# One layer half of the first group spread behind the second group's attention, in a fused gated-attention and layer kernel

## The chip, the cores and the metric

The kernel runs on one core of a Trainium2 chip. A core has a matrix engine (TensorE, PE in the profile; its weight loads are listed apart as PEld), a vector engine (VectorE, DVE), an engine for functions of one argument (ScalarE, ACT), GpSimd (POOL) and a queue engine (SyncE, SP) that here only issues DMAs. Each engine works through its own queue in order, and engines wait for one another through semaphores. The metric is the device time of one execution in microseconds; less is better.

## The reference

Two parts follow one another. The first is a recurrence over 768 steps for each of 4 x 8 heads of width 48: a complex state with a per-channel decay, written by k and v and read by q. The second is a layer over the 3072 rows that come out of it.

```python
mag = np.sqrt(a_re * a_re + a_im * a_im)
scale = np.minimum(mag, 0.999) / (mag + 1e-06)
a_re_n, a_im_n = (a_re * scale, a_im * scale)
for t in range(S):
    new_re = ar * S_re - ai * S_im
    new_im = ar * S_im + ai * S_re
    S_re, S_im = (new_re + np.einsum('bhd,bhe->bhde', k[:, :, t], v[:, :, t]), new_im)
    y[:, :, t] = np.einsum('bhd,bhde->bhe', q[:, :, t], S_re)
# x: y as 3072 rows of 384
h = x @ w_in            # 384 x 2048
g = h * np.cos(h)
out = g @ w_out         # 2048 x 384
```

All arrays are float32 but for the two weight matrices, which come as float64.

## The kernel before

**Tiles and groups.** The recurrence is computed in chunks of 128 steps. Two chunks make a group, and there are 12 groups, numbered from 0 (so that group 0 is the first). In a group, logarithms of the decays are summed along the chunk by a matmul with a triangular matrix, and their exponentials scale q and k. Angles are summed in the same way and give sines and cosines. Then a chunk is an ordinary masked attention (`f_scores`, `f_out`, L931 and L943) and a carried state (`f_state`, L984).

**The steps of a group, by their names in the code.**

- `log_steps` (L731): 3 logarithms and 3 exponentials on ScalarE, and sums and products on VectorE. It writes the tiles `lg`, `tan`, `mag` and `rs`.
- `p_powers` (L790): the matmuls `lgs` and two exponentials for each chunk; `p_even` and `p_apply` (L802, L830): five VectorE products, and a small DMA pair through `row`.
- `g_angle` (L836): an arctangent; `g_carry` (L844): only from group 2 on, the carry of the angle and its split into two halves.
- `g_phase` (L855): the matmuls `phs`, a cast on ScalarE and a subtraction on VectorE for each chunk. In groups 0 and 1 the second chunk's matmuls read the first chunk's finished phase.
- `g_trig` and `g_stack` (L869, L882): two sines, and four products that give `ks` and `qs`.
- Group 1 turns `ks` and `qs` by TensorE transposes (`f_turn`, L914, tiles `tp`). From group 2 on VectorE transposes them (`f_transpose`, L894), and a DMA through DRAM (`moved`) brings them to `kT` and `qT`.
- `f_xt` (L1003) brings the attention's output `yT` through DRAM into `xT`, the layer's input.

**The layer.** Its first half, `mm1(g, jp)`, is eight tiles of 128 x 512 a group (`hp`, 12 matmul records each). ScalarE takes a sine with a quarter turn (`gate`) and a square whose sum is kept as a check (`junk`), and VectorE multiplies: `gate` = hp cos(hp). The second half, `mm2`, multiplies the gates by `w_out` into `op`. Groups 0 and 1 do it plainly, 16 matmuls (32 records) for each of two chunks; `second(g, i)` (L1198) cuts them into four quarters. Later groups use seven products of sums in place of eight.

**The weights.** Each matrix is brought in eight parts (`into` for `w_in`, `back` for `w_out`) by DMAs that POOL issues, and turned from float64 to float32 by `as_floats` (L621): one ScalarE and three VectorE instructions a part. Four staging buffers `raw` take turns in the pool `stage`, which is closed (`room.close()`) once all parts are there. A quarter of `second` needs two parts of `w_out`.

**Buffers.** PSUM has eight banks: five in turn under the tag `a` (scores, sums, transposes), two under `m` and one under `acc` (layer). Each third `hp` tile of a group goes to `acc`. There are eight `gate` buffers.

**What sets the order.** All matmuls are chained in the order in which the code calls them, and so are ScalarE's functions that need a table (`special`, L704, which also places the table loads), the squares of the logs, and POOL's DMAs. The other instructions of VectorE and ScalarE and the DMAs on SP are placed by a planner when the program is built: among those that are ready by its own costs, the one that the code calls first. `weave` (L1140) orders the calls: each list of steps gets a stretch of 0 to 1, its steps are spread evenly over it, and all are called by position. The start (to about 45 us) is written out by hand; then come two `weave` calls for groups 0 and 1, the closing of `stage`, one more `weave`, and a loop over the other groups.

Of the kernel before, what the change touches and what calls it, by code (L numbers as in the profile page):

```python
# [11 lines left out]
F32 = mybir.dt.float32  # L12
# [475 lines left out]
def fast_path(ctx, tc, q, k, v, a_re, a_im, moe_w_in, moe_w_out, out, least, odd, wide):  # L488
# [8 lines left out]
    DM, DF = moe_w_in.shape  # L497
    C = 128
    NCH = S // C
    G = 2  # L500
# [7 lines left out]
    NJ = DF // C  # L508
# [7 lines left out]
    msb = ctx.enter_context(tc.tile_pool(name="msb", bufs=2))  # L516
# [3 lines left out]
    stage = {"pool": room.enter_context(tc.tile_pool(name="stage", bufs=1)), "bufs": 4}  # L520
    pa = ctx.enter_context(tc.tile_pool(name="pa", bufs=5, space=PSUM))
    pm = ctx.enter_context(tc.tile_pool(name="pm", bufs=3, space=PSUM))
# [20 lines left out]
    X = [dict() for _ in range(NG)]  # L543
    Y = [dict() for _ in range(N)]

    PEG, PER = 2, 1

    def load(g, names, i=None, put=nc.sync.dma_start):  # L550
        for name in names:
            ap = {"re": a_re, "im": a_im, "q": q, "k": k, "v": v}[name]
            if name not in X[g]:
                X[g][name] = ld.tile([C, G, H, D], F32, tag=name, name=name,
                                     bufs=2 if name == "v" else 1)
            b, c = divmod(g * G + (i or 0), NCH)
            one, n = i or 0, G if i is None else 1
            steps = ap[b].rearrange("h (c p) d -> p c h d", p=C)[:, ds(c, n)]
            tile_ = X[g][name][:, ds(one, n)]
            parts = [(0, C, 0)]  # L560
            if name in ("re", "im") and g >= PEG:

                parts = [(0, C - 16, 1), (C - 16, C - 1, 1)]
                put(out=tile_[C - 1:C], in_=steps[0:1])
            for i_ in range(n):
                for lo, hi, by in parts:
                    put(out=tile_[lo:hi, i_], in_=steps[lo + by:hi + by, i_])

    idle = stage["pool"].tile([C, 512], F32, name="idle")
    nc.vector.memset(idle, 1.0)  # L570
    for names in ("re", "im"), ("k", "q"), "v":
        for i in range(G):
# [15 lines left out]
    RAW = stage["bufs"]  # L588
# [115 lines left out]
    def special(func, **kw):  # L704
        preload(tables[func])
        chain(nc.scalar.activation(func=func, **kw))  # L706
# [4 lines left out]
    def temp(tag, bufs=1):  # L711
        return gt.tile([C, G * DM], F32, tag=tag, name=tag, bufs=bufs)
# [5 lines left out]
    def cut(t, i, n):  # L718
        return (flat(t) if len(t.shape) == 4 else t)[:, ds(i * DM, n * DM)]
# [70 lines left out]
    def p_powers(g, i):  # L790

        x = X[g]
        if i == 0:
            x["P"], x["Q"] = x["lg"], temp("Q")
            x["row"] = rows_d.tile([G * DM], F32, tag="row", name="row")
            x["end"] = ft.tile([D2, G * H], F32, tag="end", name="end")
        ps = pa.tile([C, DM], F32, tag="a", name="lgs")
        summed_up(ps, g, i, "lg", sums[0])
        special(out=cut(x["P"], i, 1), in_=ps, func=AF.Exp)
        special(out=cut(x["Q"], i, 1), in_=ps, func=AF.Exp, scale=-1.0)  # L800
# [35 lines left out]
    def g_angle(g, i, n):  # L836

        at = cut(X[g]["tan"], i, n)
        special(out=at, in_=at, func=AF.Arctan)
# [172 lines left out]
            out=xt.rearrange("p c g t -> p c (g t)"),  # L1012
            in_=moved.rearrange("p s d t -> (p s d) t").rearrange("(c r) t -> r c t", r=C))

    def mm1(g, jp):
        x = X[g]
        third = len(x.setdefault("gate", {})) % 3 == 2
        ps = pm.tile([C, 2, G * C], F32, tag="acc" if third else "m", name="hp",
                     bufs=1 if third else 2)
        for ji in range(2):  # L1020
            for dc in range(ND):
                matmul(ps[:, ji], lhsT=w_in[:, jp, dc, ts(ji, C)],
                       rhs=x["xT"][:, dc].rearrange("p g t -> p (g t)"),
                       start=(dc == 0), stop=(dc == ND - 1))
        gate = msb.tile([C, 2, G * C], F32, tag="gate", name="gate", bufs=8)
        junk = msb.tile([C, 2, G * C], BF16, tag="junk", name="junk", bufs=1)
        special(out=gate, in_=ps, func=AF.Sin, scale=1.0 / in_scale, bias=half_pi_b)
        scalar.activation(out=junk, in_=ps, func=AF.Square, scale=1.0 / in_scale,
                          accum_out=wide[:, ds(g * (NJ // 2) + jp, 1)])
        gated = vector.tensor_tensor(out=gate, in0=ps, in1=gate, op=ALU.mult)  # L1030
        x.setdefault("gated", gated)
        x["gate"][jp] = gate

    def mm2(g, i, j0, nj):
        if j0 == 0:
            Y[g * G + i]["op"] = pm.tile([C, DM], F32, tag="acc" if i == 0 else "m", name="op",
                                         bufs=1 if i == 0 else 2)
        ps = Y[g * G + i]["op"]
        for j in range(j0, j0 + nj):
            matmul(ps, lhsT=X[g]["gate"][j // 2][:, j % 2, ts(i, C)], rhs=w_out[:, j],  # L1040
                   start=(j == 0), stop=(j == NJ - 1))
        if j0 + nj == NJ:
            ot = msb.tile([C, DM], F32, tag="ot", name="ot")
            scalar.mul(out=ot, in_=ps, mul=1.0 / (in_scale * out_scale))
            nc.sync.dma_start(out=out[ts(g * G + i, C), :], in_=ot)
# [1 line left out]

    PLAIN, HJ, E2 = 2, NJ // 2, DM // 2  # L1050
    b11, b12, b21, b22 = (w_out[:, ds(r * HJ, HJ), ds(c * E2, E2)]
                          for r in range(2) for c in range(2))
    right = {"a11": b11, "a12": b21, "s3": b12, "s4": b22}
# [86 lines left out]
    def weave(*parts):  # L1140

        items = []
        for p, (part, lo, hi) in enumerate(parts):
            part = list(part)
            items += [(lo + (hi - lo) * (i + 0.5) / len(part), p, t)
                      for i, t in enumerate(part)]
        for _, _, t in sorted(items, key=lambda x: x[:2]):
            t()
# [4 lines left out]
    def keys(g):  # L1153

        if not 0 <= g < NG:
            return
        for i, n in spans(g):
            yield lambda i=i, n=n: g_trig(g, i, n)
            yield lambda i=i, n=n: (g_stack(g, i, n), p_end(g, i, n))
            for name in "kT", "qT":  # L1160
                if g >= PEG:
                    yield lambda i=i, n=n, name=name: f_transpose(g, i, n, name)

    def turned(g, i, name):
        return [lambda hh=hh: f_turn(g, i, name, hh) for hh in range(2)]

    def prods(g):
        if not 0 <= g < NG:
            return
        for i in range(G):  # L1170
            yield lambda i=i: p_powers(g, i)
        yield lambda: g_angle(g, 0, G)
        yield lambda: g_carry(g)
        yield lambda: (p_even(g, 0, G), p_apply(g, 0, G))

    def logs(g):
        yield from each(g_log, g)
        if 0 <= g and g + 1 < NG:
            yield lambda: load(g + 1, ("re", "im"))

    def phases(g):
        return [lambda i=i: g_phase(g, i) for i in range(G)] if 0 <= g < NG else []

    def chunks(g):
        for n in range(g * G, g * G + G):
            for hh in range(2):
                yield lambda n=n, hh=hh: f_scores(n, hh)
            yield lambda n=n: f_state(n)
            yield lambda n=n: f_out(n)
        yield lambda: f_xt(g)  # L1190
        if g + 2 < NG:
            yield lambda: load(g + 2, ("k", "q", "v"))

    def first(g):
        order = range(NJ // 2) if g < PLAIN else (0, 4, 1, 5, 2, 6, 3, 7)
        return [lambda jp=jp: mm1(g, jp) for jp in order]

    def second(g, i):  # L1198
        return [lambda j0=j0: mm2(g, i, j0, 4) for j0 in range(0, NJ, 4)] if g < PLAIN else []

    def convert(parts):
        return [lambda dst=dst, src=src: weight(dst, src)() for dst, src in parts]
# [12 lines left out]
    into, back = weight_parts()  # L1215
# [35 lines left out]
    for t in (turned(0, 0, "kT") + turned(0, 0, "qT") + early[:1]  # L1251
# [6 lines left out]
              + [lambda: next(one, None), lambda: next(two, None),  # L1258
                             lambda: load(2, ("v",))]):
        t()  # L1260
    weave((logs(1), 0.0, 0.1), (convert(into[RAW:]), 0.0, 0.5),
          (first(0), 0.2, 1.0), (prods(1), 0.55, 0.58), ([lambda: load(2, ("k", "q"))], 0.58, 0.6),
          (phases(1), 0.7, 0.8), (keys(1), 0.8, 0.9), (convert(back[:4]), 0.5, 1.0))
    over = [t for i in range(G) for name in ("kT", "qT") for t in turned(1, i, name)]
    weave((convert(back[4:]), 0.0, 0.3), (second(0, 0), 0.0, 0.65), (over, 0.2, 0.6),
          (logs(2), 0.3, 0.31), (chunks(1), 0.7, 1.0), (prods(2), 0.85, 0.87))
    room.close()
    stage.update(pool=ctx.enter_context(tc.tile_pool(name="late", bufs=1)), bufs=1)
    weave((second(0, 1), 0.0, 0.35), (phases(2), 0.2, 0.3), (keys(2), 0.3, 0.45),
          (first(1), 0.4, 1.0))  # L1270
    for n in range(2, NG):
        weave((mixes(n - 1, 2, 4), 0.0, 0.12), (logs(n + 1), 0.0, 0.02), (chunks(n), 0.0, 0.36),
              (second(n - 1, 0), 0.0, 0.38), (products(n - 1, 0, 3), 0.0, 0.36),
# [82 lines left out]
```

## Time and profile before

| what | us |
|---|---|
| median of three runs (lowest, highest) | 675.45 (675.18, 677.47) |
| the profiled execution | 674.87 |
| its span, first to last instruction | 673.0 |
| TensorE busy | 649.9 (97%) |
| VectorE busy | 490.5 (73%) |
| ScalarE busy | 396.5 (59%) |
| 26 table loads on ScalarE, 1283 ns each | 33.4 |

The profile is of one execution. Busy time is what an engine spends in its instructions; it overlaps between engines. In a line of instructions, `out<-in` are the program's tile names, followed by shapes and the count; in brackets stands the idle time of the engine just before, and the instruction that ended it. Most instructions carry the line of a helper that issues them (L686 for matmuls, L675 for VectorE and ScalarE, L706 for `special`), so the tile names tell them apart. One matmul in the code is two records in the trace (a transpose is one). The length of an instruction overlaps with the start of the next one on its engine, so that a row of equal ones is counted by its pitch.

### The profile page before, as it was taken

To read this page: it belongs to the slowest core of one execution; us is meant where nothing else is said; L and a number is where in the kernel's file an instruction comes from. 1 tells how busy PE (TensorE), PEld (TensorE's weight loads), DVE (VectorE), ACT (ScalarE), POOL (GpSimd) and SP (SyncE) were. 2 spreads that over 40 slices of the span, in tenths; PEclk is the share of its full clock that TensorE was granted. 3 is DMA by queue.
4 is the path that set the end of the run, shared out by engine and by line. 5 is a ranking of instruction groups with operands and counts; after the bars stand their busy time and mean duration, and the time that the engine had idled before them with its cause. 6 is when DMAs were issued, how large, how long until landed. Compare 5 with 4: busy or idle time off the path is not lost.

```text
span 673.0 us, 10725 instructions
## 1 busy us (share of the span) xinstructions
PE 649.9 (97%) x4055; PEld 579.6 (86%) x4055; DVE 490.5 (73%) x793; ACT 396.5 (59%) x730; POOL 27.8 (4%) x47
## 2 busy tenths in 40 slices
PE   7897899999999999999999999999999999999995
PEld 5685677886899889999899999999999999999895
DVE  4989987668867867877768778868778768862241
ACT  6779875483574575476477467467467467332330
POOL 2012000000000000000000000000000000000000
PEclk8989989999999999999999999999999999999998
DMA  9788725814824845955945864864864862363000
GB/s 252 162 244 234 188 67 116 215 41 87 220 58 92 214 119 122 230 119 118 234 119 118 216 136 117 214 138 116 218 141 116 215 140 87 115 143 105 24 6 24
DMA packets 232810, 94.90 MB, mean 141 GB/s; under 512 B 208798, under 2 KB 221217, under 8 KB 232748
## 3 DMA queue, kind: packets, MB, share of 16 engines
q1 hardware_dynamic: 226252, 68.62, 45.2%
q0 software_dynamic: 5632, 25.17, 11.4%
q8 instruction: 34, 0.56, 0.3%
q10 hardware_dynamic: 864, 0.33, 0.2%
q14 instruction: 28, 0.23, 0.1%
HBM read 69.28 MB, written 24.81 MB: 140 GB/s over the span
## 4 chain that ended last, share of the span: by engine, by line
PE 80%; ACT 6%; DVE 6%; DMA 6%; issue 2%; SPq 0%; ACTq 0%; DVEq 0%
PE hp L686 32%; PE op L686 17%; PE sum L686 14%; PE yp L686 6%; PE sc L686 5%; PE sp L686 3%; PE phs L686 2%; DMA re<-in_a_re_dram 1%; PE lgs L686 1%; ACT raw L675 1%; DMA qT<-moved 1%; DMA raw<-in_moe_w_in_dram 1%; DVE mag L675 1%; DMA raw<-in_moe_w_out_dram 1%; DVE tan L675 1%
## 5 line engine op out<-in xcount | busy, mean ns | idle before, releaser
L686 PE MATMUL hp<-xT,w_in 128*128 128x256 f32 x1152 | 253.1, 381 | 1.3 <-DVE gate L675 0.9
L686 PEld LDWEIGHTS hp<-xT,w_in 128*128 128x128 f32 x1152 | 219.9, 191 | 33.3 <-DVE gate L675 1.8
L706 ACT ACTIVATE gate<-hp,half_pi_b 128x512 f32<-128x512 f32 x96 | 65.9, 687 | 127.6 <-PE hp L686 127.6
L686 PE MATMUL op<-w_out,gate 128*128 128x192 f32 (+1 forms) x448 | 103.7, 377 | 3.1 <-DVE w_out L675 3.1
L675 DVE TENSOR_TENSOR gate<-hp,gate 128x512 f32<-128x512 f32 x96 | 65.7, 685 | 55.8 <-ACT junk L675 55.8
L686 PEld LDWEIGHTS op<-w_out,gate 128*128 128x128 f32 x448 | 75.9, 191 | 19.7 <-DVE w_out L675 4.1
L675 ACT ACTIVATE junk<-hp 128x512 bf16<-128x512 f32 x96 | 56.5, 589 | 0.0
L686 PE MATMUL sum<-t_s,s 128*128 128x192 f32 x320 | 55.4, 327 | 0.0
L686 PEld LDWEIGHTS sum<-t_s,s 128*128 128x128 f32 x320 | 52.5, 191 | 0.3 <-DVE ot L675 0.3
L675 DVE TENSOR_TENSOR atm<-sc,causal 128x512 f32<-128x512 f32 x48 | 32.8, 687 | 24.8 <-PE sc L686 24.8
L686 PE MATMUL sc<-qT,kT 96*128 96x128 f32 x384 | 49.3, 276 | 1.4 <-ACT qT L675 0.8
L686 PEld LDWEIGHTS sc<-qT,kT 96*128 96x128 f32 x384 | 47.8, 192 | 3.2 <-ACT qT L675 1.1
L675 ACT ACTIVATE ot<-sum 128x192 f32<-128x192 f32 x30 | 9.5, 319 | 49.8 <-PE sum L686 49.8
L702 ACT ACT_TABLE_LOAD x26 | 33.4, 1283 | 4.0 <-DMA ident<-ident_const 3.6
L675 DVE SCALAR_TENSOR_TENSOR ot<-op,ot 128x192 f32<-128x192 f32 x31 | 11.0, 355 | 32.5 <-ACT ot L675 23.9
L675 ACT CAST tan<-phs 128x384 int32<-128x384 f32 x24 | 11.5, 478 | 39.2 <-PE phs L686 39.2
L686 PE MATMUL yp<-atm,v 128*48 128x128 f32 x352 | 33.6, 277 | 0.0
L686 PEld LDWEIGHTS sp<-v,ks 128*96 128x96 f32 x320 | 29.7, 165 | 0.0
L686 PE MATMUL yp<-qT,state 96*48 96x128 f32 x304 | 29.7, 272 | 0.0
L686 PE MATMUL sp<-v,ks 128*96 128x48 f32 x320 | 29.6, 246 | 0.0
L686 PE MATMUL sum<-w_out,gate 128*128 128x192 f32 x160 | 29.6, 329 | 0.0
L686 PE MATMUL op<-t_a,gate 128*128 128x192 f32 x160 | 29.0, 333 | 0.0
(138 smaller groups left out, 997.2 us busy)
## 6 DMA issues: line engine op xcount, KB each, us to landing
moved<-tr SPq DMA_DIRECT2D x20, 768.0 KB
raw<-in_moe_w_in_dram POOLq DMA_DIRECT2D x16, 768.0 KB, 5.8
raw<-in_moe_w_out_dram POOLq DMA_DIRECT2D x16, 768.0 KB, 4.7
kT<-moved SPq DMA_DIRECT2D x40, 192.0 KB
qT<-moved SPq DMA_DIRECT2D x10, 768.0 KB
k<-in_k_dram SPq DMA_DIRECT2D x24, 192.0 KB
q<-in_q_dram SPq DMA_DIRECT2D x24, 192.0 KB
v<-in_v_dram SPq DMA_DIRECT2D x24, 192.0 KB
```

Source lines behind the costliest of these rows:

```text
L675: ins = getattr(self.engine, op)(**kw)
L686: chain(nc.tensor.matmul(out, **kw), "tensor")
L702: chain(nc.scalar.preload_act_table_set(table))
L706: chain(nc.scalar.activation(func=func, **kw))
```

## The change

Four edits, all in the order of the work for groups 0 and 1 (41 to 140 us of the kernel before):

- `mm1` is cut in two, `mm1_sums` (matmuls) and `mm1_gate` (ScalarE and VectorE). For group 0 four tiles' sums are called ahead, three of them before group 1's powers; gates follow after group 1's arctangent. Strings of letters say which PSUM bank each tile takes (`m`, `c` for `acc`, `a`).
- The powers of group 1 are called right behind its logs, and its two phases directly behind one another, behind two gates.
- The first four gates of group 0 have four buffers of their own in the pool `stage`, the first of them shared with the constant tile `idle` of the start. `op` of both chunks of group 0 takes the bank `acc`.
- Of `second(0, 0)` the first quarter is called between the transposes of group 1's two chunks, the second in the middle of group 1's attention, and the other two after it. Seven parts of `w_out` are converted along that attention, one before it. `second(0, 1)` comes between the halves of `first(1)`, and `stage` is closed after all of this.

```diff
-    PEG, PER = 2, 1
+    PEG, PER, PLAIN = 2, 1, 2
...
-    idle = stage["pool"].tile([C, 512], F32, name="idle")
+    idle = stage["pool"].tile([C, 2, G * C], F32, tag="first", name="idle", bufs=4)
+    idle = idle.rearrange("p a b -> p (a b)")
...
-    def mm1(g, jp):
-        x = X[g]
-        third = len(x.setdefault("gate", {})) % 3 == 2
-        ps = pm.tile([C, 2, G * C], F32, tag="acc" if third else "m", name="hp",
-                     bufs=1 if third else 2)
+    def mm1_sums(g, jp):
+        x = X[g]
+        x.setdefault("gate", {})
+        order = x.setdefault("order", [])
+        home = {0: "mmcamcmm", 1: "mmmmmmcm"}[g][jp] if g < PLAIN else "mmc"[len(order) % 3]
+        order.append(jp)
+        pool, tag, bufs = {"m": (pm, "m", 2), "c": (pm, "acc", 1), "a": (pa, "a", None)}[home]
+        ps = pool.tile([C, 2, G * C], F32, tag=tag, name="hp", **({"bufs": bufs} if bufs else {}))
...
-        gate = msb.tile([C, 2, G * C], F32, tag="gate", name="gate", bufs=8)
+        x.setdefault("hp", {})[jp] = ps
+
+    def mm1_gate(g, jp):
+        x = X[g]
+        ps = x["hp"].pop(jp)
+        if g == 0 and jp < 4:
+            gate = stage["pool"].tile([C, 2, G * C], F32, tag="first", name="gate", bufs=4)
+        else:
+            gate = msb.tile([C, 2, G * C], F32, tag="gate", name="gate", bufs=8)
...
+    def mm1(g, jp):
+        mm1_sums(g, jp)
+        mm1_gate(g, jp)
...
-            Y[g * G + i]["op"] = pm.tile([C, DM], F32, tag="acc" if i == 0 else "m", name="op",
-                                         bufs=1 if i == 0 else 2)
+            Y[g * G + i]["op"] = pm.tile([C, DM], F32, tag="acc" if i * g == 0 else "m", name="op",
+                                         bufs=1 if i * g == 0 else 2)
...
-        for i in range(G):
-            yield lambda i=i: p_powers(g, i)
-        yield lambda: g_angle(g, 0, G)
+        if g != 1:
+            for i in range(G):
+                yield lambda i=i: p_powers(g, i)
+            yield lambda: g_angle(g, 0, G)
...
-    weave((logs(1), 0.0, 0.1), (convert(into[RAW:]), 0.0, 0.5),
-          (first(0), 0.2, 1.0), (prods(1), 0.55, 0.58), ([lambda: load(2, ("k", "q"))], 0.58, 0.6),
-          (phases(1), 0.7, 0.8), (keys(1), 0.8, 0.9), (convert(back[:4]), 0.5, 1.0))
-    over = [t for i in range(G) for name in ("kT", "qT") for t in turned(1, i, name)]
-    weave((convert(back[4:]), 0.0, 0.3), (second(0, 0), 0.0, 0.65), (over, 0.2, 0.6),
-          (logs(2), 0.3, 0.31), (chunks(1), 0.7, 1.0), (prods(2), 0.85, 0.87))
+    ahead = [lambda jp=jp: mm1_sums(0, jp) for jp in range(4)]
+    gates = [lambda jp=jp: mm1_gate(0, jp) for jp in range(4)]
+    powers = [lambda i=i: p_powers(1, i) for i in range(G)]
+    later = convert(into[RAW:])
+    for t in (list(logs(1)) + later[:1] + ahead[:3] + powers + later[1:2] + ahead[3:]
+              + [lambda: g_angle(1, 0, G)] + gates[:2] + phases(1) + gates[2:] + later[2:]):
+        t()
+    weave((first(0)[4:], 0.0, 1.0), (prods(1), 0.1, 0.2),
+          ([lambda: load(2, ("k", "q"))], 0.3, 0.32),
+          (keys(1), 0.35, 0.5), (convert(back[:1]), 0.9, 1.0))
+    over = [turned(1, i, "kT") + turned(1, i, "qT") for i in range(G)]
+    opening = second(0, 0)
+    weave((over[0] + opening[:1] + over[1], 0.0, 0.2), (logs(2), 0.1, 0.11),
+          (chunks(1), 0.2, 1.0), (prods(2), 0.6, 0.62), (opening[1:2], 0.55, 0.6),
+          (convert(back[1:]), 0.0, 1.0))
+    weave((opening[2:], 0.0, 0.1), (first(1)[:4], 0.1, 0.4), (second(0, 1), 0.4, 0.7),
+          (phases(2), 0.3, 0.4), (keys(2), 0.4, 0.65),
+          (first(1)[4:], 0.7, 1.0))
     room.close()
     stage.update(pool=ctx.enter_context(tc.tile_pool(name="late", bufs=1)), bufs=1)
-    weave((second(0, 1), 0.0, 0.35), (phases(2), 0.2, 0.3), (keys(2), 0.3, 0.45),
-          (first(1), 0.4, 1.0))
```

More of the change, by code (lines that the diff above doesn't have):

```diff
@@ L1045, in mm2 @@
             nc.sync.dma_start(out=out[ts(g * G + i, C), :], in_=ot)
-    PLAIN, HJ, E2 = 2, NJ // 2, DM // 2
+    HJ, E2 = NJ // 2, DM // 2
     b11, b12, b21, b22 = (w_out[:, ds(r * HJ, HJ), ds(c * E2, E2)]
```

## The prediction

> **What bounds the kernel now.** I read the engine rows in forty slices first, to find where TensorE (PE) is not full.
>
> ```profile
> PE   7897899999999999999999999999999999999995
> DVE  4989987668867867877768778868778768862241
> PEclk8989989999999999999999999999999999999998
> ```
>
> One slice is 16.8 us. PE has holes up to about 95 us and is full from there to the end. All code that the diff touches runs between 41 and 140 us, so I cut that stretch into tens (stretch; its length; busy us of PE, weight loads, VectorE, ScalarE and GpSimd; clock; DMA).
>
> ```profile
> 40.00:50.00 10.00, 9.96 (x53) 8.38 (x53) 6.77 (x10) 9.27 (x13) 0.76 (x1) 0.83 0.70 221
> 50.00:60.00 10.00, 9.27 (x41) 7.51 (x40) 10.00 (x14) 9.95 (x19) 2.04 (x3) 1.00 0.89 234
> 60.00:70.00 10.00, 7.12 (x24) 5.01 (x24) 10.00 (x15) 8.65 (x14) 1.57 (x3) 0.83 0.71 220
> 70.00:80.00 10.00, 10.00 (x43) 7.53 (x42) 9.15 (x13) 8.15 (x15) 1.55 (x2) 1.00 0.86 187
> 80.00:90.00 10.00, 6.86 (x25) 4.28 (x24) 9.88 (x17) 6.30 (x9) 0.93 (x1) 0.83 0.42 148
> 90.00:100.00 10.00, 10.00 (x88) 8.31 (x88) 8.37 (x12) 8.80 (x15) 0.00 (x0) 1.00 0.05 20
> ```
>
> From 50 to 90 VectorE (the third figure) is full and PE is not: in this stage VectorE sets the pace. The timeline of PE shows where it pays (start, length, what; in brackets the idle time and its releaser).
>
> ```profile
> 54.76 2.86 PE L686 MATMUL hp<-xT,w_in 128*128 128x256 f32 x12 [0.73 <-DVE gate L675]
> 64.38 1.65 PE L686 MATMUL phs<-tan,turns 128*128 128x384 f32 x2 [2.88 <-ACT tan L706]
> ...
> 84.00 2.36 PE L686 MATMUL op<-w_out,gate 128*128 128x384 f32 x4 [3.14 <-DVE w_out L675]
> ...
> 106.29 8.01 PE L686 MATMUL op<-w_out,gate 128*128 128x384 f32 x24
> ...
> 126.01 13.22 PE L686 MATMUL hp<-xT,w_in 128*128 128x256 f32 x60 [0.22 <-DVE gate L675]
> 139.07 1.06 PE L686 MATMUL sc<-qT,kT 96*128 96x128 f32 x8
> ```
>
> I take the last line as the milestone: at 139.07 the scores of the third group (group 2) start, and nothing later is edited. From 45.08 to there PE owes: 192 hp records at 0.216 (96 of them take 20.72) 41.5; 64 op at 0.322 (8 take 2.58) 20.6; 32 transposes 3.5; scores 3.6, states 2.6, yp 3.8; lgs 2.0; phs, 8 at 0.33 and the third group's 1.06, 3.7. Sum 81.3 of 94.0. **12.7 us is all that reordering can win**: 7 of idle time, the rest a slow PE behind each idle time (four op records after 84.00 take 2.36, elsewhere 1.29).
>
> **What the Trainium skill says.** "TensorE: Matmul & The Clock Gate", What's actually happening: an idle window of about 3.4 us halves PE's clock, and as long a busy one restores it. The trace agrees in kind: the idle times of 2.88 and 3.14 us are each followed by some 2 us lost, that of 0.73 by 0.3. "ScalarE: Activation LUTs", What ACT_TABLE_LOAD costs: 1283 ns and a drain, 2.66 in all; the trace shows 1283 on average, and the next special begins 1.29 behind a load, so I price 1.28. "Perfetto Trace Analysis", Optimization Strategy: where the most-contended engine changes over time, interleaving the regimes may help. That is what the edit does, but it also puts VectorE work of the attention stage into the stretch where VectorE is full.
>
> **The change, part by part.**
>
> *Powers behind the logs.* Before, ScalarE loads tables at 41.09, 51.40, 59.24 and 62.19. After, logs and powers share one set, then arctan and the gates one: two loads fewer, 2.57 us of ScalarE. The three hp tiles need no free bank, so PE's 0.73 at 54.04 goes. lgs run 54.0 to 55.4, the fourth hp to 58.0. On ScalarE: exponentials (4 at 0.38) to 56.4, load 57.7, arctan 58.55. PE waits 0.5 there instead of 2.88.
>
> *Two phases in a row.* Only the second phase's sums lie between the first phase and the matmul that carries it over; before, a whole hp tile did. Sums to 60.6; the cast stands behind two gates' Sin and Square (0.58 each) and ends near 61.3, the subtraction 61.9. New wait of some 1.5 on PE; behind it in PE's queue stands every later hp tile. The four remaining hp tiles: 62.6 to 73.2 (2.6 each and 0.3 for the clock). Before, they ended at 76.4.
>
> *Keys.* Their two Sins are chained behind the sixth gate: 68.7 plus Square, then 0.75 and 0.9: 70.9. Four products at 0.87: 74.5 (before 80.4). The first eight transposes end at 75.5.
>
> *A quarter of the layer half, then attention.* One part of w_out costs VectorE 0.47 + 0.87 + 0.87 = 2.2 (starts 84.73, 85.20, 86.07, 86.94). The first is done by 71, the second behind two gates at 77.9. The quarter ends 79.2, the other eight transposes 81.0. Attention of group 1 begins there, 14.3 us earlier than before (95.3); three quarters of the half, 7.7, are owed. So far 6.6 us are won.
>
> *What VectorE must do next.* This gain is not kept. Before, the eighth part of w_out was done at 93.4, with 48.6 of the 52.3 us since 41.1 busy: there is little air. After, by the written order these stand ahead of that part: the rest of group 2's logs, six at 0.87 and one at 0.47, 5.7; four masks at 0.60, 2.4; a state, 0.9; group 2's carry 0.55, split 0.87, and five products 4.35, 5.8. Together 14.8: 93.4 + 14.8 = 108.2, less an estimated 0.8 of VectorE idle time filled: **107.4**. Step by step it is the same: second and third part near 82.8 and 90.6 around the logs (which wait for ScalarE), second quarter to 91.9, group 2's lgs 92.6, attention's last yp at 96.7; fourth and fifth conversion up to 97.2 (of those in this stretch), products to 103, the last two at 105.2 and 107.4. PE does the third quarter 96.7 to 99.3, stands some 6 us, and ends the fourth at 108.7; 0.9 more for the slow clock: 109.6. The 3.14 us wait for w_out has moved and doubled. Late next is the first layer half of group 1, all of it queued behind.
>
> *Transfer of x.* Before, the last yp ended at 106.3, x was issued at 110.41 behind the row DMA of group 2's powers (109.66) on SP's queue, and hp began at 117.76: 11.4 us, covered by 32 op records (10.3). After, only two quarters (5.2) cover it: 96.7 + 11.4 = 108.1. It hides under VectorE's delay, and costs up to 6 without it.
>
> *From there.* First half of group 1 (20.7, and 0.3 for waits), second half of group 0 (10.3), phs 1.06: 32.3. Milestone 109.6 + 32.3 = 141.9, against 139.07: +2.8. Keys of group 2 now stand behind four gates; the phases end 121.2, cast, Sins, four products and two stream transposes (2.2 each) 131.6. Before, the second transpose ended 125.4 and DMA traffic of qT died out near 136.4: 11 us. After: 142.6, 0.7 to 0.9 behind the milestone; bounds 0 and 2.5, by where the transposes land. I take 0.9.
>
> *Edits at nothing.* The gate buffers of their own: the first four gates of group 1 need none of group 0's, which second(0, 1) frees later; the shared slot's idle tile is last read at 45. Without them those gates would wait 10 us, but none is taken away. Banks: two in turn for group 1 want a gate 2.6 us after its tile; Sin, Square and product take 1.8. `acc` is held by op of group 0 for 30 us, with no other user in between. Weight DMAs on POOL stay paced by conversions; the loads of re and im for group 3 go out when the logs have read them, ahead of x on SP, 4 us of issue that would hurt only next to x.
>
> **Sum.** +2.8 + 0.9 = +3.7. The profiled execution took 674.87, its span 673.0, 1.87 around it; it lies 0.58 under the median of 675.45. Span 676.7, execution 678.6, so a median of **679.2**. About 0.5% (3.4 us) is what a measurement of this kernel can tell from no change; the forecast lies at that edge.
>
> **Rivals.**
>
> *Not slower: the planner puts conversions first.* VectorE's order is the planner's: ready work by priority. Group 2's products become ready 7 us after the fourth part, for they wait for lgs, arctan and carry; the remaining conversions and masks fill 6.5 of that. If two more conversions slip in ahead, the eighth part is done 5.2 earlier, 102.2, and x, issued before the row DMA at 98.2, lands 7.3 later, 105.5. Milestone 137.8 + 0.9: 675.0. For it: how close 6.5 and 7 are. Against: before, the row DMA went ahead of x. It decides when products start after 103.
>
> *PE-bound.* If all waits dissolve, 12.7 less the slow start at 45 (1.2) and half of the slow rest: some 9 us, 666.5. Against it VectorE's sum, from which no log and no mask can be left out: 93.4 + 9.0.
>
> *ScalarE is next.* Between 74.5 and 97 ScalarE has: six log specials, squares, Relu and split 8; eight copies 4; six carriers 5.5; table loads 2.6; exponentials, arctan, split 3.1; yT 1.1: 24 in 22.5 us. If the logs are delayed and VectorE stands behind them in queue order (as 2.7 us at 44.7 and 1.5 at 93.4), 4 to 10 us come on top: 686.
>
> **Chances.** Forecast 0.45, own range 676 to 683 (0.28 of it slower, 0.17 within 0.5%). ScalarE, 683 to 690: 0.25, slower. Conversions first, 670.5 to 677: 0.20 (0.13 same, 0.07 faster). PE-bound, 663 to 669: 0.10, faster. Faster 0.17, same 0.30, slower 0.53. The range from 669 to 687 leaves out PE-bound and the top of ScalarE's case.
>
> **What would show it.** 24 table loads instead of 26; lgs near 54, hp of group 0 ended near 73, scores of group 1 near 81 instead of 95; an idle time of 5 to 8 us ahead of an op between 97 and 107, released by w_out on VectorE; the first hp of group 1 near 109; milestone near 142.5. An op that never waits there, or hp of group 1 before 104, makes the forecast wrong; x as releaser would show the second rival half right.

## The result, and the profile after

The changed kernel is slower: 684.52 us median (683.81 to 685.35) against 675.32 (675.03 to 677.47) for the kernel before, a ratio of 1.013 (95% interval 1.0106 to 1.0154). Its profiled execution took 685.35 with a span of 683.4; before it was 674.87 and 673.0. So 10.4 us of span are to be found between the two profiled executions (the medians are 9.2 apart).

The engine rows of the changed kernel in forty slices, each now 17.1 us:

```profile
PE   7798796989999999999999999999999999999996
DVE  4979995639768768868768868868768868862251
```

PE is full from the tenth slice on (154 us), where before it was full from the sixth (84 us): the 6 of slice 7 and the 8 of slice 9 are new holes. DVE (VectorE) has its "999" in slices 4 to 6, just ahead of it. The stretches of ten, columns as in the prediction (length; busy us of PE, weight loads, VectorE, ScalarE, GpSimd; clock; DMA share and GB/s):

```profile
70.00:80.00 10.00, 5.79 (x33) 4.47 (x32) 9.20 (x14) 9.70 (x18) 0.07 (x1) 1.00 0.40 62
...
100.00:110.00 10.00, 4.33 (x31) 2.73 (x28) 9.52 (x13) 3.31 (x5) 0.00 (x0) 0.87 0.47 85
110.00:120.00 10.00, 10.00 (x34) 7.04 (x34) 2.90 (x6) 1.82 (x5) 0.00 (x0) 0.79 0.56 133
```

PE's first hole of size is from 70 to 80 and its second from 100 to 110, with VectorE at 9.2 and 9.5 of 10 in both. From 110 to 120 VectorE has only 2.9 us of work, and ScalarE 1.8. What PE waits for, from its timeline (start, length, what; in brackets the idle time ahead and its releaser):

```profile
61.88 0.91 PE L687 MATMUL phs<-tan,last 128*128 128x384 f32 x2 [1.30 <-DVE tan L676]
62.62 10.52 PE L687 MATMUL hp<-xT,w_in 128*128 128x256 f32 x48
...
79.52 4.51 PE L687 MATMUL op<-w_out,gate 128*128 128x384 f32 x8 [2.98 <-DVE w_out L676]
85.62 1.95 PE L687 MATMUL sc<-qT,kT 96*128 96x128 f32 x16
...
109.62 5.10 PE L687 MATMUL op<-w_out,gate 128*128 128x384 f32 x8 [5.67 <-DVE w_out L676]
114.55 7.93 PE L687 MATMUL hp<-xT,w_in 128*128 128x256 f32 x36
...
148.98 1.13 PE L687 MATMUL sc<-qT,kT 96*128 96x128 f32 x8 [2.18 <-issue]
```

The front went as drawn: hp of group 0 ends at 73.1. Then the first quarter of op waits 2.98 us for a part of w_out, and the last quarter 5.67 us for another; the scores of group 2 start at 148.98 against 139.07. That is 9.9 of the 10.4 us, so the loss is made inside the edited stretch. VectorE ahead of the second wait:

```profile
101.55 0.96 DVE L676 SCALAR_TENSOR_TENSOR mag<-Q,lg 128x768 f32<-128x768 f32 x1
...
107.75 0.95 DVE L676 TENSOR_TENSOR mag<-q,lg 128x768 f32<-128x768 f32 x1
108.61 0.95 DVE L676 CUSTOM_DVE_ANT_0 w_out<-raw,w_out 128x1536 uint16<-128x1536 uint16 x1
```

From 101.55 to 108.6 VectorE works on group 2's split and products, with one conversion step and one short step of the state among them; the last steps of the seventh part (the third line) and of the eighth (another of that kind, at 111.06) stand behind. The eighth part is done at 112.0 (forecast 107.4). And GpSimd (POOL), which issues the loads of w_out:

```profile
64.31 0.72 POOL L617 DMA_DIRECT2D raw<-in_moe_w_out_dram  x1 [4.64 <-DVE tan L676]
79.93 2.27 POOL L617 DMA_DIRECT2D raw<-in_moe_w_out_dram  x2 [14.89 <-DVE w_out L676]
```

It stands still for 14.89 us because all four raw buffers hold parts that VectorE has not converted. Before, a load went out at 66.33, 73.53, 77.87 and 84.50. Up to 112 us no idle time of VectorE ends on one of these loads in the changed kernel, so what the stop costs here is not shown.

### The profile page after: what moved, and what is told of

Read it like the earlier page. It is cut to its first block, busy times and chain, and to the rows that moved or that the text cites. A ratio compares the mean times of both kernels' runs of the same rounds, so it can differ in the third digit from the quotient of the medians.

```text
span 683.4 us, 10723 instructions
## 1 busy us (share of the span) xinstructions
PE 651.3 (95%) x4055; PEld 578.2 (85%) x4055; DVE 490.8 (72%) x793; ACT 392.8 (57%) x728; POOL 28.5 (4%) x47
## 4 chain that ended last, share of the span: by engine, by line
PE 78%; DVE 4%; DMA 4%; ACT 3%; issue 1%; ACTq 0%; DVEq 0%; SPq 0%
PE hp L687 33%; PE op L687 17%; PE sum L687 14%; PE yp L687 5%; PE sc L687 4%; PE sp L687 3%; PE phs L687 1%; PE lgs L687 1%; DMA qT<-moved 1%; DMA raw<-in_moe_w_in_dram 1%; DVE mag L676 1%; DMA x<-yT 1%; DMA raw<-in_moe_w_out_dram 1%; DVE atm L676 1%; DMA xT<-x 1%
## 5 line engine op out<-in xcount | busy, mean ns | idle before, releaser
L687 PE MATMUL op<-w_out,gate 128*128 128x192 f32 (+1 forms) x448 | 106.5, 385 | 8.6 <-DVE w_out L676 8.6
L687 PEld LDWEIGHTS op<-w_out,gate 128*128 128x128 f32 x448 | 77.5, 194 | 27.7 <-issue 8.2
```

What stands on the lines that cost most here:

```text
L687: chain(nc.tensor.matmul(out, **kw), "tensor")
```

## The experiments

The theories, as the expectations name them: **V**, VectorE's order makes the parts of w_out late, above all the eighth; **X**, the way of x of group 1 through DRAM is no longer covered by op and binds; **Q**, the queries of group 2 come late to their scores; **F**, the loss is made in the front, before 85 us. Medians of the kernel before, measured beside each run, lie between 674.67 and 675.72; ratios are to them.

### Group 2's products behind the last quarter

```
-          (chunks(1), 0.2, 1.0), (prods(2), 0.6, 0.62), (opening[1:2], 0.55, 0.6),
+          (chunks(1), 0.2, 1.0), (opening[1:2], 0.55, 0.6),
...
-    weave((opening[2:], 0.0, 0.1), (first(1)[:4], 0.1, 0.4), (second(0, 1), 0.4, 0.7),
+    weave((opening[2:], 0.0, 0.1), (prods(2), 0.1, 0.11), (first(1)[:4], 0.1, 0.4), (second(0, 1), 0.4, 0.7),
```

> Edit: the changed kernel with group 2's powers, carry and products called behind the last two quarters of second(0, 0), not in the middle of group 1's attention. Theory V (VectorE's order delays the last parts of w_out): the eighth part, done at 111.9 in the changed kernel, loses 5.8 us of work ahead of it and is done near 106; the first half of group 1 starts near 109.5 (0.7 of it the lgs now in front) instead of 114.55, and the time falls from 684.5 to about 679.5. Theory X (the transfer of x binds): x lands near 112 whatever VectorE does, so 682 to 684; but the row DMA is out of its way here, so X alone would also give some 4 us, and only the idle time ahead of the op and of hp tells them apart: under V the op wait (5.67) is gone or halved. Theory F (the loss is made in the front, before 85 us): no change, 684.5.

683.17 us, ratio 1.0114 (1.0091 to 1.0138). PE's timeline of this kernel, then VectorE's:

```profile
104.08 2.85 PE L687 MATMUL op<-w_out,gate 128*128 128x384 f32 x8 [1.12 <-DVE w_out L676]
...
116.08 4.26 PE L687 MATMUL hp<-xT,w_in 128*128 128x256 f32 x12 [2.61 <-DVE gate L676]
146.71 1.13 PE L687 MATMUL sc<-qT,kT 96*128 96x128 f32 x8 [1.80 <-issue]
```

```profile
111.19 0.62 DVE L676 SCALAR_TENSOR_TENSOR tan<-tan,carry 32x384 f32<-32x384 f32 x1 [6.30 <-ACT tan L707]
```

The wait of 5.67 shrinks to 1.12 and hp of group 1 starts 6.5 us earlier, at 108.02: V is right about what the wait was made of. But the powers and the arctan moved with the products, VectorE stands idle for 6.30 us until that arctan is there, and then the products share it with the first gates of group 1: hp waits 2.61 for a gate, and 12 records take 4.26 where full speed is 2.75. The scores start only 2.3 us earlier, and the median is only 1.4 lower, where V was expected to give 5. The wait moved.

### A lighter conversion

The last of the three VectorE instructions of each w_out part is left out, 0.87 us a part, so w_out's values are not the reference's. This instruction is also the one that reads what ScalarE's step of the conversion gives, so a part no longer waits for ScalarE either.

```
-        vector.tensor_tensor(out=bits, in0=bits, in1=lo, op=ALU.add)
+        if len(dst.shape) == 3 and dst.shape[-1] == 256:
+            vector.tensor_tensor(out=bits, in0=bits, in1=lo, op=ALU.add)
```

> Edit: the changed kernel with the third VectorE instruction of each of the eight w_out parts left out (the addition of the low bits, so the output is slightly off): 8 x 0.87 = 7.0 us less on VectorE, nothing else moved. Theory V: the eighth part is done 7 us earlier, 105, and the time falls to about 677.5. Theory X: hp of group 1 waits for x instead, with x as releaser, and the time falls by 2 at most, to 682.5. Theory F: only the quarter's wait at 79.5 shrinks by 1.7, 682.8.

681.4 us, 1.0097 (1.0077 to 1.0116). PE's timeline:

```profile
109.59 10.10 PE L688 MATMUL hp<-xT,w_in 128*128 128x256 f32 x36 [6.91 <-DMA xT<-x]
```

Op no longer waits for w_out (16 records run from 97.25 to 102.7), and PE then stands 6.91 us for x; behind it 36 records take 10.10 instead of 7.9. So X lies directly under V: with the wait for w_out gone, hp starts 5.0 us earlier, and not at once after op. The median falls by 3.1 us, where V was expected to give 7 and X 2 at most.

### Only the front of the change

The edits up to the weave of first(0)[4:], with the two weaves behind them, the place of the gates and the banks of op and of group 1's hp as before.

```
-          (keys(1), 0.35, 0.5), (convert(back[:1]), 0.9, 1.0))
+          (keys(1), 0.35, 0.5), (convert(back[:4]), 0.5, 1.0))
```

> Edit: only the front of the change: logs, powers, sums ahead, gates and phases as in the changed kernel, but four parts of w_out converted along it, and then the second and third weave, the banks of op and the gate buffers as before. Theory V: the work of VectorE ahead of the eighth part is that of before, so that part is done near 93 again and the time is 675.3, within 1.5. Theory F: the front itself loses, 680 or more. Rival P (PE's shorter waits are worth what they save): 672, since hp of group 0 ends 3 us earlier.

677.36 us, 1.0039 (1.0026 to 1.0051). PE's timeline, then GpSimd's:

```profile
77.17 4.51 PE L687 MATMUL op<-w_out,gate 128*128 128x384 f32 x8 [4.97 <-DVE w_out L676]
```

```profile
77.58 0.93 POOL L617 DMA_DIRECT2D raw<-in_moe_w_out_dram  x1 [13.54 <-DVE w_out L676]
```

The front alone costs 2.6 us, more than V allowed (within 1.5 of the kernel before) and less than F (680 or more). It ends hp of group 0 some four us earlier than before, and PE then waits for w_out, 4.97 us here and 2.45 and 1.81 later, while the loads stood still for 13.54 us. VectorE itself waits for two of the late loads, 0.38 us at 82.41 and 1.47 at 88.61; ahead of the first wait, of 4.97, it is the order of the conversions alone that makes the part late, since no VectorE idle time from 60 to 82 ends on a load.

### The front, with the parts of w_out put first

The last kernel, with one span moved.

```
-          (keys(1), 0.35, 0.5), (convert(back[:4]), 0.5, 1.0))
+          (keys(1), 0.35, 0.5), (convert(back[:4]), 0.0, 0.36))
```

> Edit: as in the front-only run, but the four parts of w_out that are converted along the front are called earlier there (0.0 to 0.36 in place of 0.5 to 1.0 of that weave), ahead of group 1's keys. Front-only was 2.6 above before: its eighth part was done at 95.9 instead of 93.4, since the planner put all conversions behind the keys and the four staging buffers came free late. Theory V: the parts are spread again, the eighth is done near 93 and the time is that of before, 674.7 within 1. If the front loses for another reason (its two phases in a row, its waits on PE), it stays at 677.

674.84 us, 1.0004 (0.9994 to 1.0014). GpSimd issues the loads at 67.89, 72.46, 78.61 and 80.94, with no wait over 5.5 us. PE's timeline, of an execution of 676.73 us:

```profile
79.58 5.30 PE L687 MATMUL op<-w_out,gate 128*128 128x384 f32 x8 [4.89 <-DVE gate L676]
```

The front's loss is gone, so it was the deferred conversions. Its gain is gone too: PE now waits 4.89 us for a gate, which on VectorE stands behind the conversions put first, and op starts later than in the kernel before (76.38), though hp of group 0 ends earlier (74.7 against 76.4). VectorE owes PE both the gates and the parts: with the parts late PE waited for these, with the parts first it waits for a gate, and the front is worth nothing that can be measured.

### Keys of group 2 earlier

```
-          (phases(2), 0.3, 0.4), (keys(2), 0.4, 0.65),
+          (phases(2), 0.1, 0.2), (keys(2), 0.2, 0.4),
```

> Edit: the changed kernel with group 2's phases and keys called earlier in the last of the three weaves (0.1 to 0.2 and 0.2 to 0.4 in place of 0.3 to 0.4 and 0.4 to 0.65). Theory Q (the idle 2.18 us ahead of group 2's scores at 148.98 are qT's way through DRAM, late because the keys stand behind four gates): that idle time goes, 682.3. If something else holds the scores, no change: 684.5.

682.33 us, 1.0101 (1.0081 to 1.012). PE's timeline:

```profile
147.22 1.06 PE L687 MATMUL sc<-qT,kT 96*128 96x128 f32 x8
```

No wait ahead of the scores, which start 1.8 us earlier. Q is real and worth about 2 us.

### The other half of op put ahead of hp, alone and with the lighter conversion

Both put second(0, 1) between the last quarter and first(1), as before the change, to cover x, and bring the keys forward. One keeps the conversion; in the other the third instruction of each part is left out as above.

```
-    weave((opening[2:], 0.0, 0.1), (first(1)[:4], 0.1, 0.4), (second(0, 1), 0.4, 0.7),
-          (phases(2), 0.3, 0.4), (keys(2), 0.4, 0.65),
-          (first(1)[4:], 0.7, 1.0))
+    weave((opening[2:], 0.0, 0.1), (second(0, 1), 0.1, 0.4), (phases(2), 0.25, 0.35),
+          (keys(2), 0.35, 0.5), (first(1), 0.4, 1.0))
```

> Edit: the changed kernel with only the last weave in the order of the kernel before (second(0, 1), then first(1), keys between); all w_out parts in full. Theory V: the wait for the eighth part of w_out (5.7 us) stays, for it comes ahead of that weave; only the wait for qT (2.2) goes: 682.3. Theory X (the uncovered transfer of x is what costs): 677 or less.

> Edit: as in the run with light parts (the third VectorE instruction of each w_out part left out, so the output is off), and the last of the three weaves in the order of the kernel before: all of second(0, 1), then all of first(1), with group 2's keys between. Light parts alone were bound by the transfer of x (6.91 us of wait ahead of hp). Theory V+X+Q (VectorE's late conversions first, x behind them, qT at the end): x is covered again by 10 us of op, keys are early, so the wait for x, its slow clock (2.3) and the wait for qT (2.15) go: 681.4 - 11 = about 670.5 (before is 674.7 here). If the loss was not a sum of these three, 677 or more.

With the full conversion 684.36 us, 1.0134 (1.0108 to 1.016):

```profile
109.80 5.41 PE L687 MATMUL op<-w_out,gate 128*128 128x384 f32 x8 [5.68 <-DVE w_out L676]
...
148.99 1.06 PE L687 MATMUL sc<-qT,kT 96*128 96x128 f32 x8
```

With the lighter one 672.12 us, 0.9948 (0.9928 to 0.9968):

```profile
136.96 1.06 PE L688 MATMUL sc<-qT,kT 96*128 96x128 f32 x8
```

Covering x and the queries alone gains nothing over the changed kernel, because the wait for w_out is reached first. It was expected to gain Q's 2 us as well: the wait for qT is gone, but two new ones (0.58 of op for the copy ot, 0.61 of hp for a gate) and slower rows behind them take its place. With V lightened as well, the scores start 12 us earlier than in the changed kernel. It is no version to use, since VectorE has 0.87 us less work for each part (7 in all), and the kernel before was not run with that; it shows that V, X and Q taken away together leave no loss, but not how much of V is VectorE's work and how much the wait for ScalarE that went with it.

### Attention between the halves, with the front as before

Four trials on the full computation, to put conversions ahead of group 2's logs and products and let one op run cover x. The first has everything ahead of the second weave as in the kernel before:

```
+    weave((convert(back[4:]), 0.0, 0.5), (opening[:1], 0.0, 0.1), (over, 0.06, 0.3), (opening[1:2], 0.3, 0.31),
+          (chunks(1), 0.32, 0.85), (logs(2), 0.5, 0.51), (opening[2:], 0.85, 1.0))
...
+    weave((second(0, 1), 0.0, 0.35), (prods(2), 0.25, 0.26), (phases(2), 0.43, 0.53), (keys(2), 0.53, 0.6),
+          (first(1), 0.4, 1.0))
```

> Edit: the kernel before with its front unchanged; in the second weave the attention of group 1 is called ahead of the last two quarters of second(0, 0), with all conversions called ahead of group 2's logs; group 2's products are called in the third weave. Theory V says that this is the part of the idea that is free: only 3.3 us of masks and state stand ahead of the eighth part (97 instead of 93.4), and 10 us of attention fill PE while VectorE converts. The scores of group 2 then start when their keys allow, near 136 instead of 139: 672. If attention in this place costs as such, 676 or more.

691.43 us, 1.024 (1.0221 to 1.0258). PE's timeline, and the queue of SP:

```profile
121.95 5.22 PE L686 MATMUL hp<-xT,w_in 128*128 128x256 f32 x12 [7.66 <-DMA xT<-x]
153.53 2.05 PE L686 MATMUL sc<-qT,kT 96*128 96x128 f32 x8 [6.12 <-issue]
```

```profile
108.13 0.81 SPq L1007 DMA_DIRECT2D x<-yT  x2
...
118.61 0.26 SPq L818 DMA_DIRECT2D row<-lg  x1
118.97 0.39 SPq L1011 DMA_DIRECT2D xT<-x  x1
```

Op runs 40 records from 97.85 without a wait: the order does cure V. But the second pass of x (the last line) stands in SP's queue behind two output DMAs (109.03) and the row of group 2's powers (118.61), and goes out 10.8 us after the first; the late keys cost 6.12 more.

The second moves x of group 1 to GpSimd's queue, and products, phases and keys forward:

```
+        put = nc.gpsimd.dma_start if g == 1 else nc.sync.dma_start
...
-    weave((second(0, 1), 0.0, 0.35), (prods(2), 0.25, 0.26), (phases(2), 0.43, 0.53), (keys(2), 0.53, 0.6),
+    weave((second(0, 1), 0.0, 0.35), (prods(2), 0.1, 0.11), (phases(2), 0.23, 0.3), (keys(2), 0.3, 0.4),
```

> Edit: as in the run with the attention between (691.4), and two more: group 1's x goes out and comes back through GpSimd's queue, which is empty by then, and group 2's powers and products, phases and keys are called earlier in the third weave (0.1, 0.23 to 0.3, 0.3 to 0.4). That run showed VectorE's part as forecast (op never waits, done at 114), but x stood on SP's queue behind an output and behind the row DMA (xT issued at 118.97, 7.66 us of wait ahead of hp), and the keys were late by 6.12 at the end. If these two are all, hp starts near 115 and the scores of group 2 near 136 to 137: 672 to 673, under the kernel before (674.7). If x takes as long through GpSimd, 680 or more.

677.68 us, 1.0034 (1.0022 to 1.0045), a miss:

```profile
126.50 13.22 PE L686 MATMUL hp<-xT,w_in 128*128 128x256 f32 x60 [2.39 <-DVE gate L675]
139.55 1.06 PE L686 MATMUL sc<-qT,kT 96*128 96x128 f32 x8
```

x (hp starts at 116.18 without a wait) and the queries are in time, and the gate now waits behind the two stream transposes on VectorE (121.36 to 125.8). The scores start at 139.55, 0.5 later than before the change; this execution took 676.41, and the rest of the median's 2.4 us was not followed up.

The third has only the queue of x moved, seen once:

> Edit: the run with the attention between, with only x moved to GpSimd's queue. Hp starts near 115 instead of 121.95, so about 7 us of it are won and the wait for keys grows: 691.4 falls to between 684 and 690. If the queue was not the cause, the wait for x stays.

683.19 us against 675.25, just under the 684 to 690 that were expected. hp starts at 114.57 without a wait, and the scores wait for the queries:

```profile
144.38 2.04 PE L686 MATMUL sc<-qT,kT 96*128 96x128 f32 x8 [5.35 <-DMA qT<-moved]
```

The fourth takes the front with the parts first, x on GpSimd's queue, and conversions ahead of everything:

```
+    weave((convert(back[4:]), 0.0, 0.4), (over, 0.0, 0.25), (opening[:1], 0.25, 0.26), (logs(2), 0.2, 0.21),
+          (chunks(1), 0.28, 0.8), (opening[1:2], 0.55, 0.56), (opening[2:], 0.8, 1.0))
...
+    weave((second(0, 1), 0.0, 0.35), (prods(2), 0.03, 0.04), (phases(2), 0.2, 0.27), (keys(2), 0.3, 0.42),
+          (first(1), 0.4, 1.0))
```

> Edit: the idea of the change with what the runs showed: its front with w_out parts called early (674.8 alone), then the transposes, the attention of group 1 with two quarters of second(0, 0) in it, all conversions called ahead of what waits, group 2's logs in between, but its products behind; then second(0, 1) ahead of first(1), so that x has 10 us of op over it, and x on GpSimd's queue; keys early. If VectorE's late parts, x and the keys were all that cost, nothing of the three is left, PE has its attention 10 us earlier than before, and the scores of group 2 start near 135 to 137 instead of 139: 671 to 673, under before (675.3). If a further limit is there (the chain from group 2's logs through its keys to qT, some 42 us), 675 or above.

687.03 us, 1.0175 (1.0149 to 1.0202), a miss of 14 us:

```profile
81.63 1.94 PE L922 MATMUL tp<-ident,ks 128*96 128x128 f32 x8 [8.91 <-DVE ks L676]
99.72 0.67 PE L687 MATMUL yp<-atm,v 128*48 128x128 f32 x4 [5.77 <-DVE atm L676]
```

The transposes wait 8.91 us for the keys' products, and a yp 5.77 us for a mask that stands behind group 2's logs on VectorE; the scores start at 151.11. VectorE's timeline shows why the keys' products came so late. It is busy without a gap from 68.46 to 83, and conversion steps of w_out take 8.4 us of its queue ahead of these products, against 0.9 with the front alone; the products end at 82.4 in place of 74.5. So the conversions put first delay the keys, as they delayed the gate in the front with the parts first.

### The lighter conversion with x on GpSimd's queue

> Edit: the run with light w_out parts (681.4; third VectorE instruction of each part left out, output off), with x on GpSimd's queue. There hp waited 6.91 us for x, whose second DMA stood on SP's queue behind the row DMA. If the queue is the cause, x lands near 105, the wait falls to 2 or less with its slow clock, and the time to about 674 to 676. If the way through DRAM itself takes that long, no change: 681.

680.62 us, 1.0079 (1.0055 to 1.0104). PE's timeline, then GpSimd's:

```profile
107.94 9.59 PE L688 MATMUL hp<-xT,w_in 128*128 128x256 f32 x36 [4.76 <-DMA xT<-x]
```

```profile
99.09 1.19 POOL L1010 DMA_DIRECT2D x<-yT  x2 [15.63 <-ACT yT L677]
103.40 0.75 POOL L1013 DMA_DIRECT2D xT<-x  x1 [3.12 <-DMA x<-yT]
```

This was to bring 674 to 676 and took 1.7 us off the start of hp; the median's 0.8 is within the scatter of both kernels. With nothing ahead of it in the queue, x needs from its first issue at 99.09 to 107.9, 8.8 us: 4.3 until the second pass can go out, 4.5 until it has landed. In this kernel SP's queue was only a small part of X; most is the way through DRAM.

## Why the prediction was right or wrong

**Direction and mechanism: right.** The change was to cost time because VectorE reaches the eighth part of w_out late, and it did. 24 table loads as forecast:

```profile
L703 ACT ACT_TABLE_LOAD x24 | 30.8, 1283 | 4.0 <-DMA ident<-ident_const 3.6
```

The phases' wait was 1.30 (forecast some 1.5), hp of group 0 ended at 73.1 (73.2), the keys' products at 75.4 (74.5). The wait ahead of the last quarter was 5.67 (some 6), released by w_out on VectorE. From hp's start to its end the stretch took 32.25 (32.3). That it consists of group 2's work ahead of the eighth part is shown by moving the products: with 5.8 us of work moved, the last op started 5.5 us earlier (104.08). Three of the signs named in advance did not come: scores of group 1 near 81 (85.62), hp of group 1 near 109 (114.55), the milestone near 142.5 (148.98).

**Size: off by 6.7 us of span, 3.7 forecast, 10.4 found (5.3 by the medians).** The terms of the sum:

- *The eighth part*, 107.4 forecast, 112.0 found: +4.6. The step that failed is "93.4 + 14.8 = 108.2, less an estimated 0.8 of VectorE idle time filled". The first row is the changed kernel, the second and the last line are the kernel before:

```profile
41.10:111.93 70.83, 57.61 (x325) 44.53 (x324) 64.90 (x89) 52.93 (x87) 7.42 (x9) 0.92 0.63 167
41.10:111.93 70.83, 64.05 (x346) 49.20 (x346) 64.61 (x89) 57.15 (x90) 6.85 (x9) 0.93 0.57 153
111.35 0.95 DVE L675 TENSOR_TENSOR mag<-q,lg 128x768 f32<-128x768 f32 x1
```

  By operation and tile, VectorE does the same 89 instructions here in both kernels. Before, the pile ends with the last of group 2's products, at 112.3; after, with the eighth part, at 112.0. So the change moved that part from 93.4 to the end of a pile whose length stayed, and the end could have been read from the kernel before. The forecast came out lower in two ways. It had 48.6 + 14.8 = 63.4 us of work, where 64.90 were found; 0.94 of that is the second state with its two instructions. And it left 2.9 us for idle time, where 5.93 were found, against 6.22 in the same stretch before. Of these 5.93, 3.43 lie at 48.16 and 0.76 at 71.11, waits that the kernel before had too (2.68 and 0.64); 0.73 at 88.25 and 0.42 at 103.39 lie in the chain of logs and carry that was moved. All four end on a result of ScalarE. Moved work did not fill them.
- *The slow clock after the wait*: from the eighth part to the end of op the forecast had 2.2 us (107.4 to 109.6), the trace has 2.6 (112.0 to 114.55), at a granted clock of 0.57 in that stretch (0.79 over the ten us from 110). With the part itself hp of group 1 starts 4.95 after the 109.6 forecast.
- *The queries*: 2.18 of idle time for 0.9 forecast, +1.3; the second stream transpose ended at 136.7, and the scores start 12.3 later, not 11. It is within the bounds given (0 to 2.5), and the keys put earlier took it away.
- *Behind the milestone*: 10.4 of span against 9.9, 0.5 that was not followed up.

4.6 + 0.4 + 1.3 + 0.5 is 6.8, the difference but for rounding.

**The front: wrong, and hidden by the second wait.** "The first is done by 71, the second behind two gates at 77.9" was 79.4 and 80.2: the planner put both parts' last steps behind keys and gates. So the first quarter ran from 79.52, slowly (4.51 for 2.75), to 83.9 and not to 79.2, and the attention of group 1 began at 85.62, not 81.0: 9.7 us won where 14.3 was forecast. "Weight DMAs on POOL stay paced by conversions" was put down at nothing; in truth conversions that are deferred hold the four raw buffers, and the loads stop for 14.89 us. With the front alone, deferring the conversions costs 2.6 us, order and loads together (VectorE waits 1.85 us for loads there), and putting them first takes that to zero. What the stop adds in the changed kernel is not shown.

**X: right as a second bound.** The forecast gave it "up to 6 without" VectorE's delay; without it PE waited 6.91. Its size holds; that SP's queue makes most of it, as was expected later, does not, in the lighter kernel at least.

**The rivals.** *Conversions first* did not happen: only one of the remaining conversions' steps came between the products. *PE-bound* is off: no order tried on the full computation dissolved the waits. *ScalarE is next*: ScalarE is full from 70 to 80 (9.70 of 10), but has 8.01 and 7.35 in the next two tens, so it was not the bound of the stretch it was named for; the 3 us of VectorE's idle time that the forecast left out, all ahead of results of ScalarE, are a piece of this case. The time, 684.52, falls into its range (683 to 690), but by luck: PE's waits end on VectorE's results, and Q's and the clock's part have nothing to do with ScalarE. No run made ScalarE alone lighter, so how much of that idle time comes from its queue is open.

**No version on the full computation beats the kernel before.** The front with the parts first equals it. In each other trial something queued on VectorE or SP let a new wait in: gates behind products, gates behind transposes, masks behind logs, x behind an output.

## What to carry to other kernels

When an engine is full over a stretch, moving work within it decides only who waits; sum what stands ahead of each deadline on that engine, and take over the idle time that the same work shows in the old order instead of assuming that moved work fills it. If a step goes to the end of a pile, the end of that pile in the old trace is the first estimate. A consumer put behind other work also holds its staging buffers: follow the producer's queue to the point where it has no free buffer, since here four buffers turned a deferred conversion into 15 us without a load. Before taking a wait away, look for the next one that is due within a few us of it.

## What the runs showed of the hardware

- After an idle time of 2.98 us 8 op records took 4.51, where 2.75 is full speed, at a granted clock of 0.50 from 81 to 83 us; after 6.91 us 36 hp records took 10.10, where 7.93 is, at 0.50 from 109.6 to 112. The Trainium skill, "TensorE: Matmul & The Clock Gate", What's actually happening, puts the idle window at about 3.4 us; here a shorter idle time cost about 2 us on top of itself, as much as one more than twice as long. After 2.39 us (x on GpSimd's queue, products early) 60 hp records lost nothing to speak of: 13.05 to the start of the next row, where 12.96 is full speed. The 0.73 us of the prediction lost 0.1 in the same way, not 0.3.
- With 24 table loads in place of 26, 2.57 us less of ScalarE, the front with the parts first took the same time as the kernel before. No run changed the loads alone.
- x through DRAM and back took 8.8 us with its two passes issued as soon as they could be; behind two outputs and a row in SP's queue its second pass went out 10.8 us after the first.
